# A second copy of one head's queries and keys in the other row half, and a re-ordered schedule

## The chip, the cores and the metric

The kernel runs on one core of one Trainium2 chip. A core has five engines with instruction streams of their own: TensorE (PE, matrix multiplications; PEld is its weight load), VectorE (DVE), ScalarE (ACT), GpSimd (POOL) and SyncE (SP). POOL and SP also issue DMA transfers, each into its own queue. The engines meet at semaphores. The metric is the time of one execution on the device in microseconds, lower is better; it includes a little time around the span that the profile shows.

## What is computed

Attention of two kinds over 4 sequences (batch), 8 heads, 768 positions and 64 dimensions per head, followed by a gated feed-forward block over all 3072 tokens. Heads 0, 2 and 6 see all earlier positions; the other five see the first 4 positions and a window of 64.

```python
scores = scale * np.matmul(q, k.transpose(0, 1, 3, 2))
causal = rel >= 0
stream_keep = causal & (is_sink | in_win)          # n_sink 4, window 64
mask = np.where(retr[0, :, 0, 0, None, None], full_mask, stream_mask)
scores = np.where(mask[None, :, :, :], scores, -1000000000.0)
a = np.exp(scores - np.max(scores, axis=-1, keepdims=True))
a = a / (np.sum(a, axis=-1, keepdims=True) + 1e-09)
x = np.matmul(a, v)                                # then to [3072, 512]
...
g = x @ w_gate
gelu = 0.5 * g * (1.0 + erf(g * inv_sqrt2))
ffn_out = gelu * (x @ w_val) @ w_out
res_gate = 1.0 / (1.0 + np.exp(-(x @ w_res)))
return x + res_gate * ffn_out
```

## The kernel before

**Tiling and stages.** The 3072 tokens are cut into six chunks of 512, four tiles of 128 each (`CHUNKS`, L25). A chunk can span two sequences: chunks two and five hold the last two tiles of one sequence and the first two of the next. This text counts chunks from one. Each chunk goes through the attention of its four tiles (`attention`, L722), the gate and value products with the gelu (`gate_value`, L1044), and the output products with the residual gate (`output`, L1099). The attention of a chunk is interleaved on PE with the output products of the chunk before.

**Queries and keys.** They are needed with the head dimension on the partitions. For chunks one and two, `loads_rows` (L642) loads rows and PE transposes them (L672). From the third chunk on, `loads_natural` (L696) has POOL load 128 positions of all heads into a staging tile `qks` (L551), and SP issues a DMA transpose (L710) into `qkt`. `qkt` holds, for each of queries and keys, four head pairs: (0, 2), (4, 6), (1, 3), (5, 7). The first head of a pair stands on partitions 0 to 63, the second on 64 to 127. A segment (the tiles of one sequence in a chunk) has two transposes per tile. Shifted copies of the values (`vs`, L632) are made by SP's DMA as well. The two staging tiles are used in turn, so POOL's loads for a later segment wait until the transposes out of that staging tile have landed.

**Scores.** `scores` (L788) builds the score matmuls of one pair. The contraction is over 64 dimensions, so a matmul uses one half of PE's rows: the upper or the lower, as the head stands on partitions 0 to 63 or 64 to 127. Matmuls on different halves can run at once. Scores go to PSUM banks of 512 columns, two banks to a group; ACT's exponential reads a group (L833). A streaming head needs one bank for a chunk. A head that sees everything needs one bank for the diagonal tiles and more for the earlier key tiles. For the pair (4, 6), head 4 streams and head 6 sees everything. Its first group holds one bank of each head; every further group holds two banks of head 6.

**x for the gate.** The weighted values are normalised on DVE (L1006, L1008) and go transposed into `xT`. Two of the four blocks of `xT` come by a DMA transpose that SP issues (`to_features_dma`, L1020, from the third chunk on), the other two by PE (L1030). The gate and value matmuls (L1076) run in two halves, over two blocks of `xT` each.

**What sets the order.** All work is entered as tasks into a graph (`Graph`, L185). A planner (`schedule`, L209) walks through time with a cost for each task, picks for each engine the ready task with the lowest priority number, and so fixes the order of each engine's instructions and of both DMA queues. `HINTS` (L46) overrides the priorities of some hundred tasks by number. `assign_waits` (L341) then sets the semaphore waits: an instruction that needs a transfer waits for its landing, and on SP and POOL whatever stands behind a waiting instruction in the list waits too. A change of PE from one tiling of the array to another costs the planner an extra `SWITCH`.

Of the kernel before, what the change touches and what calls it, by code (L numbers as in the profile page):

```python
# [5 lines left out]
SEQ = 768  # L6
# [12 lines left out]
FP16 = mybir.dt.float16  # L19
# [24 lines left out]


HINTS = (  # L46
    "0:39.65 1:493.12 14:469.96 398:-242.8 399:-201.03 400:-217.49 401:-77.67 405:543.9 410:-3184.9 "
    "583:533.02 585:-204.99 599:508.01 644:14.56 655:-31.08 656:-70.92 657:-3147.66 663:547.65 679:533.02 "
    "686:474.28 687:-25.49 690:1.7 691:-170.24 693:-141.72 694:-39.96 695:-202.5 698:53.9 702:20.38 "
    "706:-3046.83 710:493.09 711:169.94 714:-171.05 715:-2884.34 720:380.6 726:-201.02 727:493.29 "  # L50
    "728:-180.62 729:1551.24 732:478.51 735:2337.32 738:-2942.11 739:33.9 740:-81.33 741:-73.37 744:493.83 "
    "745:-3105.95 746:-1850.78 747:566.96 750:296.88 751:114.75 756:-3044 757:-179.11 773:1511.7 835:1504.98 "
    "874:2454.47 910:2410.34 928:2550.33 932:-2014.38 935:3337.35 944:3512.34 958:3480.32 977:2492.95 "
    "979:2505.99 986:2024.82 1004:2016.72 1018:3447.87 1021:3516.2 1091:3558.56 1092:2520.7 1095:2497.83 "
    "1107:1487.53 1136:4457.15 1151:4475.19 1164:4470.56 1236:4527.03 1254:4453.5 1282:2509 1285:4462.07 "
    "1307:5498.98 1311:5603.11 1322:5459.76 1338:5489.56 1355:4132.83 1367:5513.39 1378:4117.99 1463:6535.49 "
    "1475:1955.41 1479:6517.49 1486:6664.6 1494:6511.63 1496:5462.34 1507:6567.8 1512:6315.58 1514:5485.28 "
    "1519:5499.23 1539:5001.96 1559:6315.57 1587:6466.65 1590:6499 1633:7417.82 1638:7410.03 1639:7408.47 "
    "1665:7430.01 1682:6353.3 1684:5484.94 ~632:477.39 ~635:510 "
)  # L60

class Task:
# [40 lines left out]
class Pool:  # L103
# [7 lines left out]
    def can(self, kind, t):  # L111
        if kind in self.caps:
            h = self.held.get(kind, [])
            h[:] = [f for f in h if f is None or f > t]
            if len(h) >= self.caps[kind]:
                return False
        return any(f <= t for f, _ in self.free)
# [341 lines left out]
def build_kernel(nc, q, k, v, w_gate, w_val, w_out, w_res, out):  # L459
    assert N_SINK <= 64 and WINDOW == 64  # L460
    G = Graph(nc)
    sb = lambda name, shape, dt: nc.alloc_sbuf_tensor(name, list(shape), dt)
    many = lambda name, n, shape, dt: [sb(f"{name}{i}", shape, dt) for i in range(n)]
# [13 lines left out]
    P_vs = Pool(many("vs", 2, [128, NT - 1, NHEAD, DHEAD + 1], FP16))  # L477
    P_vk = Pool(many("vk", 2, [128, 8, DHEAD + 1], FP16))
    P_qkt = Pool(many("qkt", 2, [128, 2, NPAIR, SEQ], FP16))
    P_er = Pool(many("er", 2, [128, 4608], FP16))  # L480
    P_es = Pool(many("es", 2, [128, 1024], FP16))
    P_ek = Pool(many("ek", 1, [128, 640], FP16))
# [16 lines left out]
    def at(buf):  # L499
        if buf.pool is P_ps:  # L500
            return psum[:, buf.slot[0] * 512:(buf.slot[-1] + 1) * 512]
        return buf.pool.items[buf.slot]
# [73 lines left out]
    def batch(b):  # L576
        if b not in batches:
            B_ = B()
            B_.v, B_.vs, B_.vk, B_.qkt = Buf(P_v), Buf(P_vs), Buf(P_vk), Buf(P_qkt)
            B_.vtok, B_.vstok, B_.qtok, B_.ktok = {}, {}, {}, {}  # L580
            batches[b] = B_
        return batches[b]

    def values(b, a, z, base, each, on_engines=False):

        BB = batch(b)
        for i in range(a, z):
# [108 lines left out]
    def loads_natural(c, si, b, a, z):  # L696

        n = z - a
        BB = batch(b)
        st = Buf(P_st)  # L700
        base = -15 if c == 1 else 1000 * (c - 2) + 50
        for i in range(a, z):
            for j, src in ((1, k), (0, q)):
                def sv(i=i, j=j):
                    return at(st)[:, (j * 4 + i - a) * 512:(j * 4 + i - a + 1) * 512]
                ds = [dma("pool", base, 0.45,
                          (lambda sv=sv, o=o: lambda: sv().rearrange("p (o h d) -> p o h d", o=2, h=4)[:, o, :, :])(),
                          src[b, :, i * 128:(i + 1) * 128, :].rearrange("(h o) p d -> o p h d", o=2)[o], bufs=[st],
                          grp=("ld", b, i, j)) for o in range(2)]
                t = G.add("sp", 1.65, (lambda sv=sv, i=i, j=j: lambda e: e.dma_start(  # L710
                    at(BB.qkt)[:, j, :, i * 128:(i + 1) * 128], sv(), transpose=True))(), ds, base, bufs=[st, BB.qkt], dma=0.6, name="dT")
                for p in range(NPAIR):
                    (BB.ktok if j else BB.qtok)[p, i] = t
            if i == a:
                values(b, a, z, base, False)

    phase = {}

# [3 lines left out]
    def attention(c, segs, xbuf, xtbuf, xtoks, xttoks, l0=0, last=(), ek=None):  # L722
        tiles = [(b, i) for (b, a, z) in segs for i in range(a, z)]

        base = 1000 * c - (200 if len(tiles) < 4 and not l0 else 0)
# [3 lines left out]
        for k_, p in enumerate(order):  # L729
            P = B()  # L730
            P.heads, P.p, P.c, P.pr = PAIRS[p], p, c, base + 40 * k_
            retr = [IS_RETRIEVAL[h] for h in P.heads]


            banks = []
            for x in range(2):
                mine = [[(b, i if retr[x] else None, i, 1) for b, i in tiles]]
                rest = [(b, kt, max(a, kt + 1), z - max(a, kt + 1)) for b, a, z in segs for kt in range(z - 1)] if retr[x] else []
                for r in sorted(rest, key=lambda r: -r[3]):
                    for bk in mine:  # L740
                        if sum(y[3] for y in bk) + r[3] <= 4:
                            bk.append(r)
                            break
                    else:
                        mine.append([r])
                banks += [(g, x, bk) for g, bk in enumerate(mine)]
            size = lambda t: sum(y[3] for y in t[2])
            banks.sort(key=lambda t: (t[0], -size(t), t[1]))
            P.et = Buf(P_er if any(retr) else P_es)
            P.where, P.ready = {}, {}  # L750
            P.off = 0
            for g in range(0, len(banks), 2):
                scores(P, tiles, [t[1:] for t in banks[g:g + 2]], g, retr)
            todo.append(P)
        sinks = sink_scores(c, [t for t in tiles if t[1] > 0], base + 40 + 5, ek, 256 if l0 else 0)
        for t in ph(c, "sc")[n0:-1]:
# [3 lines left out]
        sc = ph(c, "sc")[:-1]  # L760
# [27 lines left out]
    def scores(P, tiles, banks, g, retr):  # L788
        scr = Buf(P_ps, "sc" if len(banks) > 1 or P.c else "scr")
        deps, mms = [], []  # L790
        lanes = [0.0, 0.0]
        p, pr = P.p, P.pr
        width = [sum(y[3] for y in blocks) * 128 for _, blocks in banks]
        base = [P.off, P.off + width[0]]
        for bi, (x, blocks) in enumerate(banks):
            o, w_ = bi * 512, base[bi]
            half = slice(64 * x, 64 * x + 64)
            for (b, kt, q0, nq) in blocks:
                BB = batch(b)
                deps += [BB.qtok[p, i] for i in range(q0, q0 + nq)]  # L800
                if kt is None:
                    deps += [BB.ktok[p, q0]] + ([BB.ktok[p, q0 - 1]] if q0 else [])
                    parts = [(max(0, q0 * 128 - 64 + 64 * s), q0 * 128 + 64 * s, 64, o + 64 * s) for s in range(2)]
                else:
                    deps.append(BB.ktok[p, kt])
                    parts = [(kt * 128, q0 * 128, nq * 128, o)]
                for i in range(nq):
                    P.where[x, kt, b, q0 + i] = w_ + i * 128
                for (k0, qq, w, oo) in parts:
                    mms.append((lanes[x], len(mms), BB, half, k0, qq, w, oo))  # L810
                    lanes[x] += max(w / 2400, 0.03)
                o += nq * 128
                w_ += nq * 128
        mms.sort(key=lambda m: m[0:2])

        def sc(e):
            return [e.matmul(at(scr)[:, oo:oo + w], lhsT=at(BB.qkt)[half, 1, p, k0:k0 + 128],  # L817
                             rhs=at(BB.qkt)[half, 0, p, qq:qq + w], start=True, stop=True)
                    for (_, _, BB, half, k0, qq, w, oo) in mms]
        qkts = [batch(b).qkt for b in dict.fromkeys(b for b, _ in tiles)]  # L820
        ts = G.add("pe", max(lanes), sc, deps, pr, bufs=[scr] + qkts, name=f"sc{p}")
        ts.mode = "row"
        ph(P.c, "sc").append(ts)

# [14 lines left out]
                    func=AF.Exp, scale=SM_SCALE))(), [ts], pr, bufs=[scr, P.et], fset="exp", name=f"exp{p}"))  # L839
        ph(P.c, "exp").extend(txs)  # L840
        P.off += cols
        for bi, (x, blocks) in enumerate(banks):
            for (b, kt, q0, nq) in blocks:
                for i in range(nq):
                    P.ready[x, kt, b, q0 + i] = txs[bi]
        if g:
            return

        st = {x: base[bi] for bi, (x, _) in enumerate(banks)}
        n = len(tiles)  # L850
        for xs in ([(0, 1)] if retr[0] == retr[1] else [(0,), (1,)]):
            w, L = n * 128, len(xs)
# [385 lines left out]
```

The softmax here doesn't subtract the row's maximum and nothing guards it: scores larger than these inputs give would overflow.

## Time and profile before

| what | value |
|---|---|
| time, median of 4 runs | 274.29 us (272.43 to 274.44) |
| the profiled execution's own time | 274.44 us |
| its span in the profile | 272.7 us |
| granted PE clock | 0.999 |
| PE busy | 265.0 us, 97% |
| DVE, ACT, POOL busy | 139.3, 140.7, 87.2 us |
| moved by DMA | 28.86 MB in 96842 packets |
| score matmuls (L817) | 399, 17.9 us busy |
| gate and value matmuls of 512 columns (L1076) | 544, 151.1 us busy |

Times in the profile are counted from the start of the span. A busy PE is one in which matmuls overlap: a 512-column matmul is listed with 379 ns, while in a row one starts every 216 ns. A DMA is shown where its queue issues it; its landing is when the semaphore tells that all of it has arrived. The chain of work goes back from the last instruction to whatever released each step.

### The profile page before, as it was taken

How to read it: one execution, taken by the hardware profiler on the slowest of the kernel's cores; microseconds unless marked ns; L12 is line 12 of the kernel's file. 1: busy time of each engine (PE TensorE's matmuls, PEld its weight loads, DVE VectorE, ACT ScalarE, POOL GpSimd, SP SyncE). 2: the span in 40 equal slices, each digit the busy share in tenths (PEclk: the TensorE clock that was granted, in tenths of full speed). 3: DMA queues.
4: the chain of work that ended last, by engine and by line, in shares of the span. 5: the costliest groups of instructions: out<-in, count | busy, mean ns of one | idle time of the engine just before them, and what ended most of it. 6: DMA issues, size and time to landing. Idle time of an engine off the chain costs nothing.

```text
span 272.7 us, 5673 instructions
## 1 busy us (share of the span) xinstructions
PE 265.0 (97%) x2392; PEld 138.8 (51%) x2392; DVE 139.3 (51%) x271; ACT 140.7 (52%) x217; POOL 87.2 (32%) x124
## 2 busy tenths in 40 slices
PE   7998999999999999899999999999999999999995
PEld 6776455465444446344455444455444455544444
DVE  2697135377335386434466534467543357643444
ACT  2686437885435876143775143787232878244210
POOL 8999405996918019991000000000000000000000
PEclk9999999999999999999999999999999999999999
DMA  6999999999999999999954200013200015010013
GB/s 87 166 202 207 184 180 230 165 158 150 169 169 155 155 144 223 141 173 177 143 137 81 77 0 0 2 41 79 79 0 0 0 41 79 22 57 1 0 38 118
DMA packets 96842, 28.86 MB, mean 106 GB/s; under 512 B 85424, under 2 KB 93232, under 8 KB 96816
## 3 DMA queue, kind: packets, MB, share of 16 engines
q0 software_dynamic: 70320, 14.69, 63.9%
q1 hardware_dynamic: 26496, 13.80, 28.1%
q8 instruction: 19, 0.31, 0.5%
q14 instruction: 7, 0.06, 0.1%
HBM read 29.36 MB, written 6.29 MB: 131 GB/s over the span
## 4 chain that ended last, share of the span: by engine, by line
PE 85%; DMA 8%; POOL 4%; issue 1%; DVE 1%; POOLq 0%; DVEq 0%
PE ps L1076 42%; PE ps L1121 21%; PE ps L1106 8%; DMA wg<-in_moe_w_gate_dram 5%; PE ps L817 5%; DMA xT<-x 3%; PE ps L951 3%; PE ps L941 2%; PE ps L965 1%; PE ps L1058 1%; POOL qks L551 1%; POOL va L551 1%; PE ps L1030 1%; PE ps L672 1%; PE ps L908 1%
## 5 line engine op out<-in xcount | busy, mean ns | idle before, releaser
L1090 DVE SCALAR_TENSOR_TENSOR hT<-gact,ps 128x512 f16<-128x512 f16 x68 | 46.0, 687 | 68.8 <-ACT gact L1088 57.5
L1088 ACT ACTIVATE gact<-ps 128x512 f16<-128x512 f32 x68 | 39.8, 597 | 78.4 <-PE ps L1076 78.0
L1076 PE MATMUL ps<-xT,wg 128*128 128x512 f16 x272 | 75.7, 379 | 1.7 <-DMA xT<-x 1.3
L1076 PE MATMUL ps<-xT,wv 128*128 128x512 f16 x272 | 75.4, 379 | 0.8 <-DMA wv<-in_moe_w_val_dram 0.8
L1121 PE MATMUL ps<-wo,hT 128*128 128x512 f16 (+2 forms) x312 | 70.7, 363 | 0.0
L1076 PEld LDWEIGHTS ps<-xT,wg 128*128 128x128 f16 x272 | 26.3, 98 | 33.3 <-DMA xT<-x 1.8
L1076 PEld LDWEIGHTS ps<-xT,wv 128*128 128x128 f16 x272 | 26.3, 98 | 32.0 <-DMA wv<-in_moe_w_val_dram 1.3
L1121 PEld LDWEIGHTS ps<-wo,hT 128*128 128x128 f16 x312 | 27.1, 98 | 25.5 <-issue 0.6
L833 ACT ACTIVATE er<-ps 128x1024 f16<-128x1024 f32 (+4 forms) x40 | 34.2, 891 | 10.1 <-PE ps L817 9.8
L551 POOL DMA_DIRECT2D qks<-in_k_dram x36 | 28.4, 831 | 33.0 <-DMA qkt<-qks 19.4
L551 POOL DMA_DIRECT2D qks<-in_q_dram x36 | 28.9, 847 | 0.8 <-POOLq L1220 0.8
L1125 DVE SCALAR_TENSOR_TENSOR otile<-srs,ps 128x512 f32<-128x512 f32 (+2 forms) x26 | 16.6, 644 | 18.6 <-PE ps L1121 16.1
L1106 PE MATMUL ps<-wr,xT 128*128 128x512 f16 x96 | 24.7, 380 | 0.0
L551 POOL DMA_DIRECT2D va<-in_v_dram x24 | 21.5, 952 | 2.5 <-PE ps L965 2.5
L1109 ACT ACTIVATE srs<-ps 128x512 f32<-128x512 f32 x24 | 14.3, 597 | 11.2 <-PE ps L1106 10.9
L817 PE MATMUL ps<-qkt 64*128 64x64 f16 (+3 forms) x399 | 17.9, 215 | 0.0
L1008 DVE TENSOR_TENSOR xtok<-ps,rcp 128x512 f32<-128x512 f32 (+1 forms) x28 | 16.9, 609 | 0.5
L1128 DVE TENSOR_TENSOR otile<-otile,xtok 128x512 f32<-128x512 f32 (+2 forms) x26 | 16.7, 648 | 0.6
L817 PEld LDWEIGHTS ps<-qkt 64*128 64x128 f16 x399 | 10.3, 94 | 8.8 <-issue 4.2
L1106 PEld LDWEIGHTS ps<-wr,xT 128*128 128x128 f16 x96 | 8.7, 98 | 10.7 <-issue 1.2
L1138 PE MATMUL ps<-blank 128*128 128x128 f16 x117 | 11.4, 248 | 2.0 <-DVE blank L523 2.0
L833 ACT ACTIVATE es<-ps 128x1024 f16<-128x1024 f32 (+1 forms) x14 | 12.6, 899 | 1.3 <-PE ps L817 1.3
(67 smaller groups left out, 209.8 us busy)
## 6 DMA issues: line engine op xcount, KB each, us to landing
out_dram<-otile SPq DMA_DIRECT2D x23, 256.0 KB, 2.4
va<-in_v_dram POOLq DMA_DIRECT2D x24, 128.0 KB, 18.7
qks<-in_k_dram POOLq DMA_DIRECT2D x32, 64.0 KB, 10.2
qks<-in_q_dram POOLq DMA_DIRECT2D x32, 64.0 KB, 11.1
wg<-in_moe_w_gate_dram POOLq DMA_DIRECT2D x3, 512.0 KB, 10.7
wv<-in_moe_w_val_dram POOLq DMA_DIRECT2D x3, 512.0 KB, 12.2
wo<-in_moe_w_out_dram POOLq DMA_DIRECT2D x4, 384.0 KB, 23.8
vs<-va SPq DMA_DIRECT2D x4, 260.0 KB, 6.2
```

The source lines that it names most:

```text
L551: return G.add(eng, issue, lambda e: e.dma_start(out_ap(), in_ap), deps, prio, bufs=bufs, dma=cost, name=name, grp=grp)
L817: return [e.matmul(at(scr)[:, oo:oo + w], lhsT=at(BB.qkt)[half, 1, p, k0:k0 + 128], rhs=at(BB.qkt)[half, 0, p, qq:qq + w], start=True, sto ...
L833: return e.activation(out=o, in_=i_, func=AF.Exp, scale=SM_SCALE)
L1008: t2 = G.add("dve", c_dve(2 * n * 64), lambda e: e.tensor_tensor(out=xview(), in0=avv(0, DHEAD), in1=scale(), op=ALU.mult), [t1] + xdeps, ...
L1076: return lambda e: [e.matmul(at(dst)[:, :], lhsT=w[:, ci, f * 128:(f + 1) * 128], rhs=at(xtbuf)[:, ci, :], start=(ci == 0), stop=(ci == NC ...
L1088: ta = G.add("act", c_act(512), (lambda gb=gb, ga=ga: lambda e: e.activation(out=at(ga)[:, :], in_=at(gb)[:, :], func=AF.Gelu))(), [tg], p ...
L1090: th = G.add("dve", c_dve(512), (lambda vb=vb, ga=ga, f=f: lambda e: e.scalar_tensor_tensor(out=at(h)[:, f, :], in0=at(ga)[:, :], scalar=0 ...
L1106: e.matmul(at(rb)[:, :], lhsT=at(xtbuf)[:, ci, s], rhs=wr[:, ci, :], start=(ci == 0), stop=(ci == NCB - 1))
L1109: ta = G.add("act", c_act(512), (lambda rb=rb, sr=sr: lambda e: e.activation(out=at(sr)[:, :], in_=at(rb)[:, :], func=AF.Tanh, scale=0.5)) ...
L1121: e.matmul(at(fb)[:, w], lhsT=at(h)[:, fi, s], rhs=wo[:, fi, w], start=(fi == 0), stop=(fi == NF - 1))
L1125: t1 = G.add("dve", c_dve(n), (lambda fb=fb, sr=sr, ot=ot, w=w: lambda e: e.scalar_tensor_tensor(out=at(ot)[:, w], in0=at(sr)[:, w], scala ...
L1128: t2 = G.add("dve", c_dve(n), (lambda ot=ot, lt=lt, w=w: lambda e: e.tensor_tensor(out=at(ot)[:, w], in0=at(ot)[:, w], in1=at(xbuf)[:, lt, ...
```

## The change

From the third chunk on, after the transposes of a segment SP issues one more DMA. It copies the queries and keys of pair (4, 6) from partitions 64 to 127 of `qkt`, that is head 6, to partitions 0 to 63 of a new tile `q6` (two buffers of it, one for each sequence in flight). The copy depends on all transposes of its segment.

In `attention`, the banks of head 6 behind the first are split into those whose queries and keys are all in `q6` and those that are not. They are put in an order in which one on the upper half of partitions is followed by one that reads `q6` on the lower half. In the third chunk the first two key tiles came through PE and are not in `q6`, so only the banks of later key tiles can move. `scores` chooses the half, the tile to read and the dependencies by that mark. As five tasks are new and all later numbers move, `HINTS` is replaced by another set of priorities.

```diff
@@ HINTS: all entries replaced
...
+    P_q6 = Pool(many("q6", 2, [128, 2, SEQ], FP16))
...
@@ def loads_natural
+        if BB.q6 is None:
+            BB.q6 = Buf(P_q6)
+        loaded = []
...
+                loaded.append(t)
...
+        t = G.add("sp", 0.8, lambda e: e.dma_start(at(BB.q6)[0:64, :, a * 128:z * 128], at(BB.qkt)[64:128, :, 1, a * 128:z * 128]),
+                  loaded, base + 1, bufs=[BB.qkt, BB.q6], dma=0.4, name="q6")
+        t.late = 2.0
+        for i in range(a, z):
+            BB.q6tok[0, i] = BB.q6tok[1, i] = t
@@ def attention
+                if p == 1 and x == 1:
+                    can = lambda bk: all((0, i) in batch(b).q6tok and (1, kt) in batch(b).q6tok
+                                         for b, kt, q0, nq in bk for i in range(q0, q0 + nq))
+                    left, mine = sorted(mine[1:], key=lambda bk: -sum(y[3] for y in bk)), mine[:1]
+                    low = [bk for bk in left if can(bk)]
+                    up = [bk for bk in left if not can(bk)]
+                    while up or low:
+                        mine.append((up or low).pop(0))
+                        if low or up:
+                            lower.append(id(low[0])) if low else None
+                            mine.append((low or up).pop(0))
                 banks += [(g, x, bk) for g, bk in enumerate(mine)]
             size = lambda t: sum(y[3] for y in t[2])
-            banks.sort(key=lambda t: (t[0], -size(t), t[1]))
+            if p != 1:
+                banks.sort(key=lambda t: (t[0], -size(t), t[1]))
+            else:
+                banks.sort(key=lambda t: (t[0], -size(t) if not t[0] else 0, t[1]))
...
-                scores(P, tiles, [t[1:] for t in banks[g:g + 2]], g, retr)
+                scores(P, tiles, [t[1:] + (id(t[2]) in lower,) for t in banks[g:g + 2]], g, retr)
@@ def scores
-            half = slice(64 * x, 64 * x + 64)
+            lane = 0 if low else x
+            half = slice(64 * lane, 64 * lane + 64)
             for (b, kt, q0, nq) in blocks:
                 BB = batch(b)
+                if low:
+                    q6s.add(BB.q6)
+                    deps += [BB.q6tok[0, i] for i in range(q0, q0 + nq)] + [BB.q6tok[1, kt]]
...
-            return [e.matmul(at(scr)[:, oo:oo + w], lhsT=at(BB.qkt)[half, 1, p, k0:k0 + 128],
-                             rhs=at(BB.qkt)[half, 0, p, qq:qq + w], start=True, stop=True)
-                    for (_, _, BB, half, k0, qq, w, oo) in mms]
+            side = lambda BB, low, j: at(BB.q6)[:, j, :] if low else at(BB.qkt)[:, j, p, :]
+            return [e.matmul(at(scr)[:, oo:oo + w], lhsT=side(BB, low, 1)[half, k0:k0 + 128],
+                             rhs=side(BB, low, 0)[half, qq:qq + w], start=True, stop=True)
+                    for (_, _, BB, half, k0, qq, w, oo, low) in mms]
```

Instructions issued by SP before and after the change, in order, up to the third chunk's transpose of x (T: transpose into `qkt`, vs: shifted values, out: results, q6: the new copy, xT: the transpose of x):

| | SP's list |
|---|---|
| before | 5 vs, out, T, out, 4 T, out, 2 T, out, T, vs, 8 T, 2 vs, 4 T, 2 vs, 2 out, xT |
| changed | 5 vs, T, 2 out, 7 T, 2 out, vs, T, q6, 7 T, 2 vs, T, q6, 3 T, out, 2 vs, q6, xT |

## The prediction

> **What bounds the kernel now.** I read the page's head and its table of 40 slices first, then the waits, then the chain of work that ended last, and at the one place where that chain leaves TensorE, the timelines of PE and SP.
>
> The page (busy time and share of each engine, the slices, the chain's shares):
>
> ```profile
> span 272.7 us, 5673 instructions
> PE 265.0 (97%) x2392; PEld 138.8 (51%) x2392; DVE 139.3 (51%) x271; ACT 140.7 (52%) x217; POOL 87.2 (32%) x124
> PEclk9999999999999999999999999999999999999999
> DMA  6999999999999999999954200013200015010013
> PE 85%; DMA 8%; POOL 4%; issue 1%; DVE 1%; POOLq 0%; DVEq 0%
> ```
>
> TensorE is the bound, at a granted clock of 0.999. The DMA engines are loaded through the first 20 slices, to about 136 us; this matters below.
>
> PE's own waits (who waited, for whom, total us, times, longest):
>
> ```profile
> PE ps L1138 <- DVE blank L523: 2.0, 1, 2.0
> PE ps L1076 <- DMA xT<-x: 1.3, 1, 1.3
> PE ps L1076 <- DMA wv<-in_moe_w_val_dram: 0.8, 1, 0.8
> PE ps L1076 <- DMA wg<-in_moe_w_gate_dram: 0.5, 1, 0.5
> PE ps L672 <- DMA qks<-in_q_dram: 0.4, 1, 0.4
> ```
>
> After the third piece of wg (28.6 us) PE waits once: for the transposed x of the third chunk, xT. The timeline of PE there, and that of SP, whose queue issues this transpose (start us, length us, what):
>
> ```profile
> 111.69 1.03 PE L1076 MATMUL ps<-xT,wv 128*128 128x512 f16 x4
> 113.98 0.60 PE L1076 MATMUL ps<-xT,wg 128*128 128x512 f16 x2 [1.26 <-DMA xT<-x]
> ...
> ```
> ```profile
> 96.04 6.33 SPq L710 DMA_TRANSPOSE qkt<-qks  x4
> 102.41 1.23 SPq L632 DMA_DIRECT2D vs<-va  x2
> 103.68 1.11 SPq L1132 DMA_DIRECT2D out_dram<-otile  x2
> 104.84 2.82 SPq L1021 DMA_TRANSPOSE xT<-x  x1
> ```
>
> Four matmuls at 0.216 us from 111.69 end at 112.55, so the stall is 1.43 us. SP works its list in order; the x for this transpose was ready at 101.9 (DVE L1006 starts at 101.25, 0.68 long), yet it went out at 104.84 behind other copies, and landed 9.1 us later, at 113.93:
>
> ```profile
> 104.84 9.10 DMA xT<-x
> 113.93 0.05 issue
> 113.98 2.12 PE ps L1076 x9
> ```
>
> So from here on, the end of the kernel is this landing plus PE's remaining work. Whatever PE saves before 113.98 only lengthens the stall, unless the landing moves too.
>
> **The change part by part.** The sum stands against the profiled execution, 274.44 us (span 272.70 and 1.74 around it), 0.15 above the median of 274.29.
>
> *Scores.* In chunks three to six, six groups of pair (4, 6) put two banks of head 6 on one row half. In the chain these take 0.76 and 0.66 us (chunk three, at 90.76 and 93.60), 0.66 (132.28), 0.77 (172.53), 0.76 and 0.66 (216.43, 219.27). A group of two full banks over both halves takes 0.55 (99.14, pair (0, 2)). Six groups at 0.55 save 0.21+0.11+0.11+0.22+0.21+0.11 = 0.97; counting the columns of each half gives 0.94, as some last banks are short. 0.31 lies before the stall, 0.63 behind it. The exponentials keep their sizes.
>
> *The new priorities* reorder everything. Comparing the two instruction lists between the wait for the third wg piece and the wait for xT, the changed kernel has six gate matmuls fewer, 6 x 0.216 = 1.30, besides the 0.31 of scores. It reaches the xT wait 1.61 earlier, at 110.9, if the wg piece lands as before; POOL issues the weight pieces in the same order and only the causal mask's two short instructions (0.23 and 0.31) move. Behind the xT wait stand four gate matmuls more (0.86) and 0.63 less of scores: 0.23 longer. Four warm-up matmuls more fall into the start, which waits for loads, and cost nothing; if that cover were gone, 4 x 0.06. Before the wg wait PE does some 0.4 of gate work more, in what were its stalls of 0.8 and 0.5.
>
> *The copies.* Five q6 copies join SP's list, 0.6 of issue each (the vs copies of the same size, 130 KB, take 0.59). Each first waits until all transposes of its segment have landed, and everything behind it on SP stands. Three go out before the third chunk's xT. The first waits for the eighth transpose of chunk three's queries and keys (landing 9.0 in before), the second for chunk four's last (7.2), the third for the last of chunk five's first segment. Only that third one is directly ahead of xT. Before, nothing ahead of xT waited for a landing that SP itself had just started.
>
> The landings of qkt transposes over the whole run, and of the one issued at 90.6 with nothing queued in front (two answers on line 710):
>
> ```profile
> DMA to landing us min/median/max: 2.5/7.5/10.6
> ...
> ```
> ```profile
> DMA to landing us min/median/max: 6.7/6.7/6.7
> ```
>
> Walk: the segment's last transpose is issued at X. In before X = 101.1. Its load (issued 86.49, 13.3 to landing) is there at 99.8, so X cannot be much earlier; if the second copy waits until 100.4 (93.19 + 7.2), three transposes at 1.3 behind it put X at 103.6. I take 101.1. The wait is 4.4 (the row issued at 101.09) to 7.9 (the one at 91.88). I take 6.7: in the changed order POOL's loads for the next segment are released by chunk four's transposes, which end earlier because those loads no longer stand behind values, so they are in flight here, as at 90.6. The out and two vs copies between lie inside this wait. SP is free at 107.8, issues q6 until 108.4, and xT then, 3.6 later than before.
>
> xT's own landing: 9.1 in its row, but there behind two vs and two out copies, the last of which landed 5.9 after 104.32, at 110.2, 3.7 before xT. Now it stands behind one copy: 107.8 + 4.4 (the vs rows at 102.4 and 103.0: 3.9 to 5.0) + 3.7 = 115.9. With the whole 9.1 it is 117.5. I take the middle, 116.7: 2.8 later than 113.93.
>
> Sum: 274.44 + 2.77 + 0.23 = **277.4 us**. PE's 1.61 is swallowed: the stall grows from 1.43 to 5.8.
>
> [...]
>
> Ends of the walk: X = 99.8, wait 4.4, q6 landing 4.4 later, then 3.7: xT at 112.3, 273.0 us. X = 103.6, wait 7.9, 0.6, 9.1: 121.2, 281.9 us.
>
> *What else could stall.* The first q6 must land before chunk three's scores (90.7): issued about 81, at most 9 later, 90. A miss of a microsecond there is swallowed by the xT stall as well. The next xT was issued at 143.76, landed in 3.7, and PE used it at 153.37: 5.9 of room, and the fifth q6 ahead of it waits about 4.1 after 135.1. No loss taken.
>
> **The rivals.**
>
> *No change.* The copies' waits fall into time in which SP idled anyway: SP's waits show 6.3 us for one load of q before 90.64. The load order of the changed kernel removes this idle time. If that pays for the waits, xT goes out at about 105 and lands within 112.5 to 115: 273.1 to 275.7, say 274.4.
>
> *Faster.* POOL now issues chunk four's sixteen query and key loads before its values (in before, five of them after a wait of 2.5 for PE and behind four values), and its first loads of chunk three may start 5.6 earlier. If the loads and not the DMA engines' capacity set the pace, the whole SP list moves forward. Turning point: xT at 113.7. If it lands by 110.9 the stall is gone: 274.44 - (113.98 - 110.9) + 0.23 = 271.6. Against: the DMA row shows no free slice there, and one less late load leaves the same bytes to move.
>
> *The pairing does nothing on the array.* Then 0.94 is lost; only 0.63 of it would show: 278.0, inside the forecast's case. Against: two matmuls on different halves start 3 ns apart (96.262 and 96.265 in the trace), on one half 216.
>
> **How the numbers follow.** Forecast (xT after 115.1, a loss over 0.5%) 0.66; no change 0.17; faster 0.17. One measurement of this kernel can tell about 0.5%, 1.4 us, from no change. The ends of the walk, 273.0 and 281.9, shortened above by 0.4 as all its high values at once are unlikely, leave out under 2 in 10. The forecast's own range is 275.8 to 281.5.
>
> **What would show it.** Right: the wait of PE for xT grows to about 6 us, starting near 111; SP's timeline shows a gap of 4 us or more before the third q6; xT lands at 115 to 119; the six score groups take 0.55 each. Wrong: xT issued before 106, or a stall of PE at another place than this, or the third piece of wg landing more than 1 us away from 28.6, which moves everything behind it.

## The result and the profile after

The changed kernel takes 274.59 us (median of 43 executions, 272.18 to 279.06), the kernel before 272.66 us (64 executions beside them, 271.49 to 278.69). The ratio is 1.0043 with a 95% interval of 1.0024 to 1.0061: slower, as forecast, but by 0.4% and not by the 1.1% that 277.4 stands for. (The ratio leaves out executions more than 1.5% above the fastest of their kernel, the medians hold all.) The profiled execution took 274.89 us.

The page of the changed kernel (busy time and share of each engine, the clock and DMA slices, the chain's shares):

```profile
span 273.1 us, 5690 instructions
...
PE 266.3 (98%) x2396; PEld 139.8 (51%) x2396; DVE 140.4 (51%) x270; ACT 140.4 (51%) x218; POOL 87.4 (32%) x124
...
PEclk9999999999999999799999999999999999999999
DMA  6999999999999999999944200013200015200013
...
PE 77%; DMA 13%; SPq 6%; DVE 1%; issue 1%; ACT 0%; POOL 0%; DVEq 0%; POOLq 0%
```

Two things are new against before: DMA and SP's queue make 19% of the chain, where DMA had 8% and SP's queue none, and one slice of the clock row, the seventeenth, shows 7 in place of 9. PE's waits (who, for whom, total us, times, longest):

```profile
PE ps L1110 <- DMA xT<-x: 2.8, 1, 2.8
PE ps L1172 <- DVE blank L525: 1.1, 1, 1.1
```

The waits for the weight pieces at the start are gone, and the wait for the third chunk's xT is 2.8 where it was 1.3. The chain there (start us, length us, what; the wait of SP and its end):

```profile
101.20 5.51 DMA qkt<-qks
...
106.79 0.64 SPq L724
...
107.47 4.79 DMA xT<-x
112.26 0.05 issue
112.31 20.85 PE ps L1110 x88
```

This is the forecast's chain of causes, link by link: the last transpose of the third copy's segment goes out at 101.20; SP stands until it has landed, at 106.71; then the third q6 copy (L724, which the profile names `q<-qkt`), then xT, on which PE waits. The same place on PE's timeline, and in windows of time (from, to, length, then busy time of PE, PEld, DVE, ACT and POOL, the granted clock, the DMA share and GB/s):

```profile
108.90 0.59 PE L1110 MATMUL ps<-xT,wg 128*128 128x512 f16 x2
112.31 3.43 PE L1110 MATMUL ps<-xT,wg 128*128 128x512 f16 x8 [2.81 <-DMA xT<-x]
115.53 1.66 PE L1110 MATMUL ps<-xT,wv 128*128 128x512 f16 x6
```
```profile
110.00:112.30 2.30, 0.00 (x0) 0.00 (x0) 0.59 (x1) 0.00 (x0) 2.30 (x4) 1.00 1.60 175
112.30:116.00 3.70, 3.69 (x10) 1.34 (x11) 0.00 (x0) 1.43 (x3) 3.70 (x6) 0.54 1.81 194
116.00:120.00 4.00, 4.00 (x20) 1.81 (x19) 1.23 (x2) 1.15 (x3) 4.00 (x6) 1.00 1.87 188
```

The two matmuls from 108.90 end at 109.33 by their 0.216 us each; PE then stands for 2.98 us. When it starts again its clock is at 0.54 of full speed until 116: eight matmuls need 3.22 us to the next group's start where 8 x 0.216 = 1.73 would do. Narrower windows show where it begins and ends:

```profile
112.30:113.30 1.00, 0.99 (x3) 0.41 (x4) 0.00 (x0) 0.09 (x1) 1.00 (x3) 0.61 1.47 231
113.30:114.30 1.00, 1.00 (x4) 0.34 (x3) 0.00 (x0) 0.74 (x2) 1.00 (x2) 0.50 1.65 212
114.30:115.30 1.00, 1.00 (x4) 0.39 (x3) 0.00 (x0) 0.36 (x1) 1.00 (x2) 0.50 1.93 176
115.30:116.30 1.00, 1.00 (x5) 0.34 (x3) 0.00 (x0) 0.53 (x1) 1.00 (x2) 0.69 2.21 145
```

Before, PE stood for 1.43 us at this place and its clock stayed at 1.00:

```profile
113.90:115.00 1.10, 1.02 (x5) 0.51 (x6) 0.00 (x0) 0.38 (x1) 1.10 (x2) 1.00 1.85 179
```

This second loss is in no step of the prediction.

### The profile page after: what moved, and what is told of

Read it like the earlier page. It is cut to its first block, busy times and chain, and to the rows that moved or that the text cites. A ratio compares the mean times of both kernels' runs of the same rounds, so it can differ in the third digit from the quotient of the medians.

```text
span 273.1 us, 5690 instructions
## 1 busy us (share of the span) xinstructions
PE 266.3 (98%) x2396; PEld 139.8 (51%) x2396; DVE 140.4 (51%) x270; ACT 140.4 (51%) x218; POOL 87.4 (32%) x124
## 4 chain that ended last, share of the span: by engine, by line
PE 77%; DMA 13%; SPq 6%; DVE 1%; issue 1%; ACT 0%; POOL 0%; DVEq 0%; POOLq 0%
PE ps L1110 36%; PE ps L1155 17%; DMA qks<-in_k_dram 6%; PE ps L1140 6%; SPq L717 5%; DMA qkt<-qks 5%; PE ps L851 4%; PE ps L1172 4%; PE ps L1092 3%; PE ps L985 2%; DMA xT<-x 2%; PE ps L676 2%; PE ps L975 2%; PE ps L999 1%; PE ps L1064 1%; PE ps L942 1%
## 5 line engine op out<-in xcount | busy, mean ns | idle before, releaser
L1110 PE MATMUL ps<-xT,wv 128*128 128x512 f16 x272 | 73.8, 380 | 0.0
L851 PE MATMUL ps<-qkt 64*128 64x64 f16 (+4 forms) x391 | 16.8, 213 | 0.0
L1172 PE MATMUL ps<-blank 128*128 128x128 f16 x121 | 12.0, 254 | 1.1 <-DVE blank L525 1.1
```

What stands on the lines that cost most here:

```text
L851: return [e.matmul(at(scr)[:, oo:oo + w], lhsT=side(BB, low, 1)[half, k0:k0 + 128], rhs=side(BB, low, 0)[half, qq:qq + w], start=True, sto ...
L1110: return lambda e: [e.matmul(at(dst)[:, :], lhsT=w[:, ci, f * 128:(f + 1) * 128], rhs=at(xtbuf)[:, ci, :], start=(ci == 0), stop=(ci == NC ...
L1172: G.add("pe", 0.06, lambda e, warm=warm: e.matmul(at(warm)[:, 0:128], lhsT=blank[:, :], rhs=blank[:, :], start=True, stop=True), [t_blank] ...
```

## The experiments

### The kernel before, once more

The same code, for how typical its first profile was.

> The kernel before once more, for a second profile of it. If its first profile was an ordinary execution, the third piece of wg lands near 28.6 us again, PE waits about 1.4 us for the third chunk's xT at 112.6, and the span is near 272.7. If that execution was a late one at its start, the piece lands near 26.9 as in the changed kernel's profile, and the span is 1 to 2 us shorter, at 270.7 to 271.7, with no low clock anywhere.

Measured: 273.3 us (271.77 to 275.23, 12 executions), ratio 1.0023 [0.9988, 1.0058]; the profiled execution 272.49 us, span 270.8. PE's waits beside the one at the start, and SP's queue ahead of xT:

```profile
PE ps L1076 <- DMA wg<-in_moe_w_gate_dram: 0.7, 1, 0.7
```
```profile
100.29 1.23 SPq L632 DMA_DIRECT2D vs<-va  x2
101.56 1.14 SPq L1132 DMA_DIRECT2D out_dram<-otile  x2
102.75 2.11 SPq L1021 DMA_TRANSPOSE xT<-x  x1
```

Here xT goes out 2.1 us earlier than in the profile that the prediction was made from, lands at 111.58, and PE does not wait for it. The stall of 1.43 belonged to an execution that was late on SP. It was not late in the way that was expected: the third piece of wg landed at 28.07 here, against 28.59, and not near 26.9. In the first profile 272.70 - 113.98 = 158.72 us lay behind the stall; counted back from this span PE comes to the place at 270.8 - 158.72 = 112.08, half a microsecond after the landing.

### The third copy behind xT

```diff
+    xD = [t for t in G.tasks if t.name == "xD"]
+    q6 = [t for t in G.tasks if t.name == "q6"]
+    q6[2].order.append(xD[0])
...
     span = G.schedule()
```

Only SP's list changes: xT's transpose stands ahead of the third copy, and some transfers behind it change places. PE, DVE, ACT and POOL keep the lists of the changed kernel.

> The changed kernel with one thing moved: the third q6 copy stands behind the third chunk's xT on SP. PE, DVE, ACT and POOL keep their orders. Theory A (the copy's wait for its transposes holds xT back, PE's stall of 3.0 us grows long enough for the clock to drop afterwards, and that is the loss): xT is issued near 105.1 instead of 107.5, PE waits 0 to 1.5 us instead of 3.0, the granted clock stays at 1.00 behind it, and the time falls by 2 to 4 us against the changed kernel, to or below the kernel before (ratio to it 0.993 to 1.000). Theory B (the new priorities lose the time, wherever SP stands): the time stays within 0.2% of the changed kernel, ratio 1.004.

Measured: 270.52 us (270.28 to 272.12, 11 executions), ratio to before 0.9916 [0.9885, 0.9946]. SP's queue and PE's chain:

```profile
101.59 0.58 SPq L1166 DMA_DIRECT2D out_dram<-otile  x1
102.22 1.12 SPq L636 DMA_DIRECT2D vs<-va  x2
103.39 2.16 SPq L1055 DMA_TRANSPOSE xT<-x  x1
...
112.17 0.79 SPq L724 DMA_DIRECT2D q<-qkt  x1
```
```profile
108.89 0.43 PE ps L1155 x2
109.32 19.43 PE ps L1110 x90
128.75 0.38 PE ps L942 x8
```

xT goes out at 103.39 and not at 107.47, lands at 109.06, and PE runs through without a wait and at a clock of 1.00. The position of one copy in one queue turns a loss of 0.4% into a gain of 0.8%. So the loss comes from where the third copy waits, ahead of xT, with the stall and the half clock that follow from it. This version beats both kernels. On another chip, beside the next experiment:

> The version with the third copy behind xT, once more, as the yardstick for the kernel with its pairing switched off, on the same chip. Both theories: 270.3 to 270.8 us, no wait of TensorE for xT, clock 1.00.

Measured: 271.47 us (270.51 to 272.73), ratio 0.9936 [0.9903, 0.9968], above the 270.3 to 270.8 that were expected, with a wait for xT of 0.3 us in the profile, and 0.6 for a weight piece that landed 0.45 later (27.63 and not 27.18).

### The same without the pairing

```diff
-                    mms.append((lanes[lane], len(mms), BB, half, k0, qq, w, oo, low))
+                    mms.append((lanes[lane], len(mms), BB, slice(64 * x, 64 * x + 64), k0, qq, w, oo, low))
...
-            return [e.matmul(at(scr)[:, oo:oo + w], lhsT=side(BB, low, 1)[half, k0:k0 + 128],
-                             rhs=side(BB, low, 0)[half, qq:qq + w], start=True, stop=True)
+            return [e.matmul(at(scr)[:, oo:oo + w], lhsT=side(BB, False, 1)[half, k0:k0 + 128],
+                             rhs=side(BB, False, 0)[half, qq:qq + w], start=True, stop=True)
```

> The version with the third copy behind xT, with the five copies and every priority kept, but head 6's second bank of each pair goes over its own row half again (it reads qkt, not q6). TensorE no longer waits for xT in this version, so what the array loses must show whole. Theory (two banks on different halves run side by side): six groups grow back by 0.97 us in all, to 271.5 us from 270.5. Rival (the pairing does nothing on the array): 270.5 us. Copies that cost TensorE's loads or the DMA engines something are in both and don't show.

Measured: 271.85 us (271.24 to 273.2), ratio to before 0.9956 [0.9926, 0.9986]; against the yardstick 271.47. Here are the busy times of PE and PEld in the score matmuls from the third chunk on (85 to 235 us; sum and mean over four windows), for the kernel before, the changed kernel and this one:

```profile
sum 150.00, PE 11.73 PEld 6.76; mean PE 2.93 PEld 1.69
```
```profile
sum 150.00, PE 10.78 PEld 6.36; mean PE 2.69 PEld 1.59
```
```profile
sum 150.00, PE 11.74 PEld 6.83; mean PE 2.94 PEld 1.71
```

On PE the pairing saves 11.74 - 10.78 = 0.96 us, within 0.01 of the theory's 0.97; switched off, all of it comes back. In the time it shows as 0.4 us by the medians; the two intervals overlap, so the size of that is not settled. The yardstick waited 0.3 us for xT in its profile, so a part of what pairing saves ahead of that place was lost there.

### The copies under the old priorities

The changed kernel with the priorities of the kernel before, counted without the five new tasks:

```diff
@@ HINTS: the entries of the kernel before
...
+    numbered = [t for t in G.tasks if t.name != "q6"]
     for x in "".join(HINTS).split():
         n_, p_ = x.split(":")
-        setattr(G.tasks[int(n_.strip("~"))], "swap" if n_[0] == "~" else "prio", float(p_))
+        setattr(numbered[int(n_.strip("~"))], "swap" if n_[0] == "~" else "prio", float(p_))
```

> The copies and the pairing with the priorities of the kernel before (each priority at the task it had there). Theory A: the copies' waits on SP cost here too, as three copies stand ahead of xT: xT is issued at 107 to 110, PE stalls 2 to 6 us, the clock drops behind it, ratio 1.005 to 1.02. Theory B: as the old order is kept, the pairing's 0.6 to 0.9 us are gained, ratio 0.996 to 0.999.

Measured: 281.53 us (279.25 to 283.32), ratio 1.0295 [1.0241, 1.0349]. SP's queue ahead of xT, PE's waits, and the clock behind the stall (windows):

```profile
109.92 0.63 SPq L723 DMA_DIRECT2D q<-qkt  x1
110.60 0.59 SPq L1165 DMA_DIRECT2D out_dram<-otile  x1
111.23 1.37 SPq L1054 DMA_TRANSPOSE xT<-x  x1
```
```profile
PE ps L1109 <- DMA xT<-x: 4.5, 1, 4.5
PE ps L1171 <- DVE blank L524: 2.0, 1, 2.0
PE ps L1063 <- DVE x L1039: 1.4, 2, 1.1
PE ps L1109 <- DVE xT L1070: 1.2, 2, 0.6
```
```profile
116.40:118.00 1.60, 1.45 (x4) 0.57 (x5) 0.00 (x0) 0.52 (x1) 1.60 (x4) 0.61 1.71 157
118.00:120.00 2.00, 2.00 (x6) 0.76 (x5) 0.69 (x1) 0.08 (x1) 2.00 (x3) 0.50 1.84 220
120.00:122.00 2.00, 2.00 (x11) 0.86 (x9) 0.00 (x0) 0.53 (x1) 2.00 (x3) 0.96 1.84 164
```

Without new priorities the copies cost some 9 us, more than either expectation had: xT goes out 3.8 us later still (111.23 against 107.47), the stall (4.7 us) and the half clock are there, and PE waits for DVE at places where it did not wait before. The new priorities bring back 7 of the 9 us.

### The new priorities without copies and pairing

```diff
+        last_dT.append(t)
...
+    numbered = []
+    for t in G.tasks:
+        numbered.append(t)
+        if t in last_dT:
+            numbered.append(None)
...
```

The first line stands in `loads_natural`, behind each segment's transposes; the empty places keep the numbers of the changed kernel, where the copies stand.

> The priorities of the changed kernel (each at the same task), without copies and without pairing. Theory A: nothing on SP waits for a landing ahead of xT, xT goes out as soon as its x is ready, near 102 to 105, PE waits 0 to 1.5 us, no low clock, ratio 0.996 to 1.003 (the pairing's 0.9 us is not gained). Theory B: the loss is still there, ratio 1.004 to 1.008.

Measured: 273.5 us (273.27 to 274.53), ratio 1.0025 [0.9994, 1.0057]. xT goes out at 102.83 and lands at 107.92; PE does not wait for it, but 0.7 and 0.6 us for DVE on the way. The planner builds another list from the same priorities when the copies are missing (behind 108.59, PE alternates here between two wg and two wv matmuls, where the changed kernel has eight of wg and six of wv in a row), so this is no measure of the changed kernel's list; it only tells that the priorities showed no gain by themselves.

### Filling the stall

Is the half clock an effect of PE having stood still? Into the changed kernel's list, between the last matmul ahead of the wait for xT and the wait, go matmuls that add zeros to the bank in work:

```diff
     span = G.schedule()
+    xD = [t for t in G.tasks if t.name == "xD"][0]
+    at_ = next(i for i, t in enumerate(G.prog["pe"]) if xD in t.deps)
+    tb = G.prog["pe"][at_ - 1]
+    tb.fn = (lambda fn, buf: lambda e: list(fn(e)) + [
+        e.matmul(at(buf)[:, 0:128], lhsT=blank[:, :], rhs=blank[:, :], start=False, stop=False) for _ in range(52)])(tb.fn, tb.bufs[0])
```

> The changed kernel with 52 matmuls of 128 columns that add zeros (52 x 0.054 = 2.8 us) put in front of the wait for xT, so that TensorE is busy from 109.5 to 112.3; SP's and all other lists are the same, xT lands as before at about 112.3. Theory (the half clock after the stall comes from TensorE having been idle for 3 us): granted clock 1.00 behind 112.3, the eight matmuls there take 1.73 in place of 3.43, and the run is 1.7 us shorter than the changed kernel: 272.9 us, ratio to before 0.6% lower. Rival (the half clock comes from something else at that time, such as the DMA traffic or the landing): clock 0.5 behind 112.3 again and 274.6 us, or more where the zeros outlast the landing.

> As the kernel with the filled stall, but 24 matmuls (1.3 us), which leave a stall of about 1.6 us, near the 1.43 after which the kernel before showed a clock of 1.00. Theory (only an idle time of more than some 1.5 to 3 us lowers the clock): clock 1.00 behind the stall and the same time as with the filled stall, 272.9 us, since xT's landing sets both. Rival (any idle time there lowers it): half clock behind the stall, 274.6 us.

Half filled (24 in place of 52), PE's timeline and chain:

```profile
109.67 1.50 PE L1222 MATMUL ps<-blank 128*128 128x128 f16 x24
112.36 1.90 PE L1110 MATMUL ps<-xT,wg 128*128 128x512 f16 x8 [1.18 <-DMA xT<-x]
114.09 1.46 PE L1110 MATMUL ps<-xT,wv 128*128 128x512 f16 x6
```
```profile
112.31 0.05 issue
112.36 19.17 PE ps L1110 x88
131.52 0.38 PE ps L942 x8
```

This is a clean comparison with the changed kernel: xT lands at 112.31 against 112.26, and the same 88 matmuls behind it take 19.17 us against 20.85. The half clock costs 1.68 us, which is 3.36 us at half speed. The profiled executions took 273.14 and 274.89. Filled whole, PE runs from 111.32 at a clock of 1.00; in that profile the third wg piece had landed at 28.90, PE came late, and the zeros ended 0.7 us after xT's landing, so that they cost time of their own. The medians are 273.26 us (half filled, ratio to before 1.0036 [1.0002, 1.007]) and 273.87 us (filled, 1.002 [0.9991, 1.005]): against the changed kernel's 274.59 the expected 1.7 us is not there in full, and as the intervals of the three ratios overlap, the times alone show no gain. What the half clock costs is shown by the profiles. Part of the gain had to be missing, since not all executions of the changed kernel have the half clock:

> The changed kernel once more, for how often its stall of about 3 us brings the half clock: it did so in 27 of 44 executions (mean clock 0.988 to 0.994, median 275.1 us) and not in 17 (0.999 or 1.000, median 272.9 us). Theory (idle time alone decides): about 6 in 10 again, the two groups 1.7 to 2.2 us apart. Rival (a property of the first chip): nearly all of one kind.

> As the kernel with the half-filled stall, but 12 matmuls of zeros (0.65 us), so that about 2.3 us of stall are left. With none (3 us left) 27 of 44 executions had the half clock, with 24 (about 1.6 left) 1 of 12. Theory (the longer the idle time, the likelier the half clock): between the two, 2 to 6 of 12, median 273 to 274.5 us. Rival (a fixed threshold near 3 us): none or one of 12, 273.2 us as with 24.

The changed kernel again, on another chip: 274.15 us (272.64 to 275.75), ratio 1.0011 [0.9971, 1.005], too wide to tell from before. With 12 matmuls of zeros: 274.34 us (272.17 to 276.72), ratio 1.0021 [0.9982, 1.0059]. In its profile a stall of some 2.1 us brought the half clock:

```profile
109.53 0.83 PE L1222 MATMUL ps<-blank 128*128 128x128 f16 x12
112.32 3.18 PE L1110 MATMUL ps<-xT,wg 128*128 128x512 f16 x8 [1.97 <-DMA xT<-x]
```

The mean clock of each execution tells whether a half clock fell into it (0.994 or less) or not (0.999 or more), though not where:

| zeros ahead of the wait | stall by the profile, us | executions with the half clock |
|---|---|---|
| none, priorities of before | 4.7 | 6 of 6 |
| none | 3.0 and 2.7 | 32 of 56 |
| 12 | 2.1 | 5 of 12 |
| 24 | 1.4 | 1 of 12 |
| 52 | none | 1 of 12 |

The longer the stall in the profile, the more executions have the half clock; 24 zeros are not told from 52. The kernel before has it too, in 6 of 100 executions, all of 276.9 us and more; the single ones in the last two rows (276.58 and 279.16 us) look like these. A threshold near 3 us is out (the profile with 12 zeros has the half clock after 2.1 us), and so is a property of one chip (5 of 12 without zeros in the last runs). The first 44 executions of the changed kernel fall into two groups: 27 at 274.1 us and above (median 275.1), 17 mostly below (median 272.9, one pair at 274.6 and 274.7). The second group is at the level of the kernel before, 272.66.

The traces hold the time of each change of the clock, and these tell more than the table. In the changed kernel's profile PE has full speed from 6.70 to 112.51, which is 105.813 us, then half speed for 3.413 us, then full speed again for 157.013 us, to 272.94, behind its last work. In the first profile of before full speed lasts 266.240 us, from 5.69 to 271.93, again to behind the last work. These lengths are 31, 1, 46 and 78 times 3.413 us, to 0.03 us. So in these two traces the clock changes at the edges of steps of 3.413 us, and the first edge stands 6.70 and 5.69 us behind the span's start. With the priorities of before, the windows above put the half speed from 116.75 to 120.16, 3.41 us; and in all four profiles with the half clock the 88 matmuls behind the stall take 20.85 us, against 19.17 with 24 zeros.

In the step just before the half clock, from 109.10 to 112.51 in the changed kernel's profile, PE was idle for the 2.98 us of its stall. The stall of 1.43 in the first profile of before lies in one step as well, from 111.51 to 114.92, and full speed follows. At the end of the two profiles, where PE's work is done, half speed follows a step with 2.7 us of idle time (changed) and one with 2.0 (before). If idle time counts by the step, a stall that an edge cuts in the middle would count for less; this is the author's reading, and no run tests it. How much of the shares in the table comes from that, and how much from stalls of another length, stays open, as the other executions have no profile. In the filled one PE came 2 us later than in the changed kernel's, and xT 1.3 us later.

## Why the prediction was right in sign and wrong in size

The step that failed is the landing of xT. The prediction had xT land 8.3 us after its issue; it took 4.8, behind a wait of 5.5 where 6.7 was taken, and so xT landed at 112.26 and not at 116.7. That is the low end of the prediction's own walk, 112.3, which it priced at 273.0. A second term was put at nothing without a reason: the clock behind a long stall, 1.68 us. Without this term the measured sum below would stand at 273.16, under its base of 274.44, and the executions without the half clock are at the level of the kernel before. The forecast's sign thus came right by a term that it did not have, which is luck; its chain of causes was not.

**The scores: right.** Six groups at 0.55, 0.97 saved; measured 11.73 - 10.78 = 0.95. The rival "the pairing does nothing" is out.

**The chain of causes: right.** The third copy alone stands directly ahead of xT and makes SP wait for a landing that SP has just started. X, the issue of its segment's last transpose, was taken at 101.1 and was 101.20. With the copy behind xT the loss is gone.

**The landings: the mis-sized terms.** The wait was taken as 6.7 and was 5.5 (101.20 to 106.71), in the given bounds of 4.4 to 7.9. xT's own landing was taken from 108.4 to 116.7, 8.3 us, and was 4.8, which is the larger error. In four profiles with this list xT lands 4.4 to 4.8 us after its issue. The rows used for the forecast (9.1, and 4.4 + 3.7) came from a queue with output and value copies still under way. When xT goes out in the changed kernel, two value copies and the third q6 copy are still under way too (they land at 107.95, 108.43 and 108.89), and yet it lands after 4.8. In four others it lands after 3.6 and 5.7 (the two runs with the third copy behind xT), 5.1 (without copies) and 5.3 us (priorities of before). The two slow landings, 9.1 and 8.8, are those in the two profiles of before. When xT went out in the first of these, five of SP's transfers and five of POOL's were under way; in the changed kernel's profile there were three and one. No run tests whether one of these numbers is the cause. The third copy is of 64 KB by the trace's DMA view and not of 130 as the prediction had it, and lands 2.1 us after its issue:

```profile
q<-qkt SPq DMA_DIRECT2D x1, 64.0 KB, 2.1
```

The two copies of 128 KB ahead of it landed after 7.4 and 4.7 us, and the wait for the transpose was 5.5.

**PE's arrival: early by another 1.6.** 112.55 - 1.61 = 110.9 was forecast, under the condition that the third wg piece lands at 28.6. It landed at 26.93, and PE came at 109.33. The prediction named this as what would move everything; the piece landed at 26.93, 27.18, 27.63 and 28.67 in four profiles with new priorities and at 28.59 and 28.07 in the two of before, so one profile was no basis for it. The stall was 112.31 - 109.33 = 2.98 and not 5.8.

**The half clock: missing.** It adds 1.68. A forecast of a 5.8 us stall should have asked what PE's clock does after it; the prediction counted idle time at its length alone.

**Behind xT: nearly right.** 0.23 more was forecast; 273.1 - 112.31 - 1.68 = 159.11 against 158.72 is 0.39.

**The sum with measured terms.** 274.44 + (112.31 - 113.98) + 0.39 + 1.68 = 274.84, against 274.89 in the profiled execution. The landing alone would have made it 1.67 less than the profiled execution of before; the clock gave it back.

**The base: a late execution.** The sum stood on an execution of 274.44 with a stall of 1.43, 0.15 above the median of the four times known then. Over 64 executions the median is 272.66, and the second profile has no stall. From that profile the account is: PE came to the place at 112.08 and now goes on at 112.31 (+0.23), 0.39 more behind it, 1.68 for the clock, together 2.30, which is the difference of the spans, 273.1 - 270.8. PE's whole gain ahead of the place, 112.08 - 109.33 = 2.75 us, is eaten by the stall of 2.98. Of this gain 1.14 us is the earlier wg piece (26.93 against 28.07), which is not the change's.

**The rivals.** "No change", 274.4, has the number but not the reason: its xT would go out at 105. "Faster", with its turning point "If it lands by 110.9 the stall is gone", is what the version with the third copy behind xT does: landing at 109.06, 270.5 us against the 271.6 that was worked out.

## What to carry to other kernels

A transfer that must wait for another transfer belongs behind everything urgent in its queue, not ahead of it: one such copy, moved behind one transpose, made 0.4% of loss into 0.6 to 0.8% of gain here, with every compute engine's list the same. PE's waits of 2.1 us and more brought the half clock here, in 5 of 12 executions where the profile showed 2.1, in 32 of 56 where two showed 2.7 and 3.0, and in 6 of 6 where it showed 4.7: when such a wait is forecast, add the half clock behind it to the price (1.68 us here). And before a sum is built on a stall in one profile, ask whether the landing it hangs on is the same in other executions.

## What was not expected of the hardware

Behind a stall PE's granted clock was at half speed for 3.413 us in the changed kernel's trace, which cost 1.68 us. There and in the first profile of before the clock changes at the edges of steps of that length. The profiles with a stall of 2.1, 2.7, 3.0 and 4.7 us have the half clock behind it, those with 1.4 us (24 zeros) and 1.43 us (before) do not. The same list of instructions has executions with the half clock (32 of 56) and without it; where the steps lie can be one reason, which no run tests.

The same transpose landed 3.6 to 5.7 us after its issue in eight profiles, and after 8.8 and 9.1 in the two of before. With five of SP's and five of POOL's transfers under way at its issue it took 9.1 (the first profile of before), with three and one 4.8 (the changed kernel's); whether these numbers decide it stays open. A price read from one landing in one profile is therefore uncertain by several microseconds here.
